# Fused attention and soft-MoE on one core: routing pieces moved ahead of the attention products, a new tail load, a new setup order, a new end and a whole-row relu

## The chip, the cores and the metric

The kernel runs on one core of one Trainium2 chip. The metric is the device time of one execution in microseconds (us). Runs of a kernel are compared in rounds with runs of the kernel before on the same chip. A ratio is the mean time of one kernel's fast runs over the mean of the other's fast runs of the same rounds, so it is not quite the ratio of the medians that stand beside it; the brackets are its 95% interval.

With one core a run is called slow when it is over 1.5% above the fastest of its kernel.

In the profile's lines PE is TensorE and PEld its loading of weights, DVE is VectorE, ACT ScalarE, POOL GpSimd and SP SyncE; a q behind one (ACTq) marks its issuing of loads. L90 is a line of the kernel that was profiled, so numbers shift between kernels. "Granted clock" (PEclk, in tenths on a page) is the share of TensorE's full clock that it was given.

The span in a profile is about 1.7 us shorter than the time of the same run.

## The reference, cut to what matters

```python
# q, k, v: [8 batches, 8 heads, 576, 64]; beacon_k, beacon_v: [8, 8, 16, 64]
k_all, v_all = concat([beacon_k, k]), concat([beacon_v, v])      # along the tokens
a = softmax(mask(q @ k_all.T / 8))                               # causal, beacons always seen
x = (a @ v_all) as [4608 tokens, 512]
logits = x @ phi                                                 # [4608, 32 slots]
d = softmax over the tokens;  slot_input = d.T @ x               # "slot sums"
for e in range(8):                                               # 4 slots each
    slot_out[e] = relu(slot_input[e] @ w1[e]) @ w2[e]            # 512 -> 1024 -> 512
c = softmax over the slots;   out = c @ slot_out                 # [4608, 512]
```

## The kernel before

The loop runs over 32 pairs of heads, four to a batch. In iteration `n` TensorE computes scores of pair `n` (four steps, each followed by ScalarE's exponential), the attention products of pair `n - 1`, and the transposes of q and k for pair `n + 2`. Routing of finished batches is strewn in as pieces: transposes of x, logits, transposed weights, slot sums. The weights of the experts (32 loads of 512 KB) come in during the loop.

```python
for n in range(NP):                      # NP = 32, b = batch, g = pair in the batch
    score(n, 0); score(n, 1)
    ...                                  # n == 0: turning of V, tail, loads 5 and 6
    if n >= 2: xt_piece(n - 2)           # transposes x
    if n >= 1: attend(n - 1)
    score(n, 2)
    if n + 2 < NP:
        transp(n + 2)                    # q and k; same two PSUM buffers as the pieces
        ...
    score(n, 3)
    if n >= 5 and g == 1: logit_piece(b - 1, 0)
    if n >= 6 and g == 2: logit_piece(b - 1, 1)
    if n >= 6 and g == 3: dt_piece(b - 1)
    if n >= 8 and g == 0: si_piece(b - 2)
    ...
# V's last 80 keys ("the tail"), three loads of 32 rows for four batches
def load_tail(b4, i):
    lo = (TK * (16 + i) - Nb) * D
    w = min(TK * D, S * D - lo)
    nc.gpsimd.dma_start(out=vlast[32 * i:32 * i + 32, 0:w],
                        in_=vrows[32 * b4:32 * b4 + 32, lo:lo + w])
...
# relu of an expert's hidden layer: PSUM read in order, two rows written in turn
nc.scalar.activation(hs[e][:, :, :].rearrange("p r f -> p f r"),
                     hpv.rearrange("p (f r) -> p f r", r=2), AF.Relu)
```

The softmax here doesn't subtract the row's maximum and nothing guards it: scores larger than these inputs give would overflow.

## Time and profile before

| | before |
|---|---|
| time, median of the first 3 runs | 213.06 us (210.86 to 216.03) |
| span of the profiled run (fast) | 214.2 us |
| first mask of the fifth iteration starts | 34.03 us |
| iterations 13 to 28, mean | 4.52 us |
| first mask of the last iteration starts | 156.13 us |
| last attention product to first expert layer | 5.89 us |
| expert layers | 21.6 us |
| end of the layers to the end of the span | 27.5 us |

GpSimd's causal mask of 128x1024 follows the first exponential of every iteration, so its 32 starts are a pace-maker: their distance is what an iteration takes. The stages are told with the lines in the prediction.

### The profile page before, as it was taken

How to read it: one execution, taken by the hardware profiler on the slowest of the kernel's cores; microseconds unless marked ns; L12 is line 12 of the kernel's file. 1: busy time of each engine (PE TensorE's matmuls, PEld its weight loads, DVE VectorE, ACT ScalarE, POOL GpSimd, SP SyncE). 2: the span in 40 equal slices, each digit the busy share in tenths (PEclk: the TensorE clock that was granted, in tenths of full speed). 3: DMA queues.
4: the chain of work that ended last, by engine and by line, in shares of the span. 5: the costliest groups of instructions: out<-in, count | busy, mean ns of one | idle time of the engine just before them, and what ended most of it. 6: DMA issues, size and time to landing. Idle time of an engine off the chain costs nothing.

```text
span 214.2 us, 7748 instructions
## 1 busy us (share of the span) xinstructions
PE 155.8 (73%) x3400; PEld 113.4 (53%) x3400; DVE 135.3 (63%) x268; ACT 133.6 (62%) x187; POOL 92.0 (43%) x182
## 2 busy tenths in 40 slices
PE   2438796888868788887877888888886877688200
PEld 1326675767756666665666666677564343233000
DVE  4378589578748878967875797787463121289400
ACT  2226386688767678867767876887851743389300
POOL 8426367645775643756643673346640000000000
PEclk9999699799999999999999999999997555899955
DMA  6999999999999999999999999977999300059996
GB/s 175 269 284 369 242 195 256 252 257 260 311 250 250 271 258 259 314 251 271 259 262 262 281 240 254 205 140 148 197 213 214 67 0 3 0 220 416 416 424 286
DMA packets 20273, 50.88 MB, mean 238 GB/s; under 512 B 5392, under 2 KB 5392, under 8 KB 19216
## 3 DMA queue, kind: packets, MB, share of 16 engines
q0 software_dynamic: 8000, 21.75, 52.3%
q1 hardware_dynamic: 12096, 28.35, 36.9%
q8 instruction: 26, 0.43, 0.7%
q10 hardware_dynamic: 144, 0.29, 0.4%
q14 instruction: 7, 0.06, 0.1%
HBM read 62.69 MB, written 9.44 MB: 337 GB/s over the span
## 4 chain that ended last, share of the span: by engine, by line
PE 39%; DVE 32%; DMA 9%; ACT 6%; issue 6%; SPq 1%; POOL 1%; DVEq 0%; ACTq 0%
PE av L282 12%; DVE xb L290 9%; DVE qT L244 7%; PE sc L255 7%; DMA arena<-in_k_dram 5%; DVE arena L513 5%; PE tr L305 4%; PE tr L316 4%; DMA arena<-in_moe_w_dram 4%; PE av L483 3%; ACT ex L261 3%; DVE vh L135 3%; DVE r L289 3%; ACT hbuf L470 2%; DVE kT L244 2%
## 5 line engine op out<-in xcount | busy, mean ns | idle before, releaser
L261 ACT ACTIVATE ex<-sc 128x1024 f16<-128x1024 f32 (+3 forms) x128 | 103.8, 871 | 36.0 <-PE sc L255 35.2
L263 POOL TENSOR_SCALAR_AFFINE_SELECT ex<-ex 128x1024 f16<-128x1024 f16 x32 | 35.0, 1093 | 62.3 <-ACT ex L261 62.3
L255 PE MATMUL sc<-qT,kT 64*128 64x128 bf16 (+5 forms) x576 | 42.7, 254 | 4.7 <-POOL kT L235 3.0
L282 PE MATMUL av<-vh,ex 128*128 128x65 f16 (+1 forms) x896 | 38.6, 200 | 1.2 <-issue 1.2
L282 PEld LDWEIGHTS <-ex 128*128 128x128 f16 (+2 forms) x960 | 37.0, 110 | 1.9 <-issue 1.6
L242 PE MATMUL tr<-idb,arena 64*64 64x64 bf16 x1152 | 26.9, 198 | 7.7 <-DMA arena<-in_q_dram 3.7
L242 PEld LDWEIGHTS <-arena 64*64 64x64 bf16 x1152 | 22.6, 113 | 15.5 <-issue 9.1
L290 DVE TENSOR_TENSOR xb<-av,r 128x640 f16<-128x640 f32 x32 | 26.4, 824 | 1.1
L244 DVE COPY qT<-tr 128x576 bf16<-128x576 bf16 x32 | 23.9, 747 | 4.6 <-PE tr L242 4.5
L255 PEld LDWEIGHTS <-kT 64*128 64x128 bf16 (+1 forms) x576 | 19.6, 100 | 13.0 <-issue 6.5
L244 DVE COPY kT<-tr 128x576 bf16<-128x576 bf16 x32 | 23.9, 747 | 1.0 <-PE tr L242 1.0
L309 DVE COPY xT<-tr 128x592 f16<-128x592 f16 x32 | 14.6, 456 | 14.4 <-PE tr L305 14.4
L135 DVE STREAM_TRANSPOSE vh<-vbuf 128x512 f32<-128x512 f32 x16 | 17.8, 1128 | 1.5 <-DMA arena<-in_v_dram 1.5
L164 POOL DMA_DIRECT2D arena<-in_moe_w_dram x32 | 17.8, 557 | 0.0
L289 DVE RECIPROCAL r<-av 128x10 f32<-128x10 f32 x32 | 7.1, 220 | 16.3 <-PE av L282 16.3
L316 PE MATMUL tr<-xT,phih 128*128 128x288 f16 x64 | 10.4, 284 | 8.6 <-DVE qT L244 8.4
L111 POOL DMA_DIRECT2D vbuf<-in_v_dram x28 | 15.7, 567 | 0.0
L305 PE MATMUL tr<-idh,xb 128*128 128x128 f16 (+1 forms) x160 | 14.6, 223 | 1.0 <-DVE xb L290 0.9
L320 ACT ACTIVATE eLh<-tr 128x288 f16<-128x288 f32 x16 | 6.6, 412 | 13.6 <-PE tr L316 13.6
L511 ACT ACTIVATE arena<-fp,rc 128x512 f32<-128x512 f32 x18 | 11.3, 685 | 4.0 <-PE fp L509 3.3
L477 DVE COPY hbuf<-tr 128x256 f16<-128x256 f16 x8 | 2.3, 292 | 17.1 <-PE tr L476 17.1
L305 PEld LDWEIGHTS <-xb 128*128 128x128 f16 (+1 forms) x160 | 9.4, 100 | 6.8 <-issue 5.7
(67 smaller groups left out, 152.0 us busy)
## 6 DMA issues: line engine op xcount, KB each, us to landing
arena<-in_moe_w_dram POOLq DMA_DIRECT2D x32, 512.0 KB, 9.4
arena<-in_q_dram SPq DMA_DIRECT2D x32, 288.0 KB, 9.2
arena<-in_k_dram SPq DMA_DIRECT2D x31, 288.0 KB, 11.2
out_dram<-arena SPq DMA_DIRECT2D x8, 1024.0 KB, 8.5
vbuf<-in_v_dram POOLq DMA_DIRECT2D x31, 128.0 KB, 7.5
out_dram<-arena SPq DMA_DIRECT2D x2, 512.0 KB, 3.0
arena<-in_v_dram POOLq DMA_DIRECT2D x4, 128.0 KB, 8.4
arena<-in_k_dram ACTq DMA_DIRECT2D x1, 288.0 KB, 2.8
```

The costliest lines, as they stand in the source:

```text
L111: nc.gpsimd.dma_start(out=vbuf[b % 2][32 * qd:32 * qd + 32, :], in_=bass.AP(tensor=v.tensor, offset=v.offset + lo, ap=[hs_, cs_, [1, TK * ...
L135: nc.vector.transpose(out=dst[:, e], in_=src.bitcast(FP).rearrange("p (j e) -> p e j", j=TK)[:, e])
L164: nc.gpsimd.dma_start(out=arena[:, wloc[m]:wloc[m] + WP], in_=src)
L242: nc.tensor.transpose(tp[po:po + 64, j, :], hi, idb[po:po + 64, po:po + 64])
L244: nc.vector.tensor_copy(out=dst[:, Nb:Nb + S].rearrange("p (s j) -> p s j", j=J), in_=tp[:, :, :].rearrange("p j s -> p s j"))
L255: nc.tensor.matmul(sc[0:kn, a, col:col + un], kT[n % 3][64 * a:64 * a + 64, P * c:P * c + kn], qT[n % 3][64 * a:64 * a + 64, u0:u0 + un], ...
L261: nc.scalar.activation(ex[n][:, :, o:o + w], sc[:, :, 0:w], AF.Exp, scale=scale)
L263: nc.gpsimd.affine_select(out=ex[n][:, :, 0:512].rearrange("p a (c t) -> p a c t", c=4), in_=ex[n][:, :, 0:512].rearrange("p a (c t) -> p ...
L282: nc.tensor.matmul(av[0:m, a, i * DD:(i + 1) * DD], ex[n][0:kn, a, o:o + m], vchunk(b, 2 * g + a, c, kn), start=(c == 0), stop=(c == i))
L290: nc.vector.tensor_tensor(out=xb[b % 2][:, :, 2 * g:2 * g + 2, :].rearrange("p i a d -> p a i d"), in0=avv[:, :, :, 0:D], in1=r5[:, :, :]. ...
L305: nc.tensor.transpose(tp[:, i, 0:m], xb[b % 2][0:m, i, 2 * g:2 * g + 2, :].rearrange("p h d -> p (h d)"), idh[0:m, 0:m])
L316: nc.tensor.matmul(lp[:, 0:w], phih[:, t, :, :].rearrange("p g s -> p (g s)"), xT[b][:, t, Nb + hf * w:Nb + (hf + 1) * w], start=(t == 0), ...
```

## The change

It is meant to take the routing pieces out of the wait for the q and k copies, to shorten the last batch's routing and the layers, and to start loads with fewer instructions. Cut to its core:

```diff
 def load_tail(b4, i):
-    lo = (TK * (16 + i) - Nb) * D
-    w = min(TK * D, S * D - lo)
-    nc.gpsimd.dma_start(out=vlast[32 * i:32 * i + 32, 0:w],
-                        in_=vrows[32 * b4:32 * b4 + 32, lo:lo + w])
+    rows = bass.AP(tensor=v.tensor, offset=...,
+                   ap=[[TK * D, 2], [S * D, 32], [1, TK * D]])
+    if i == 0:
+        nc.gpsimd.dma_start(out=vlast[0:64, :], in_=rows)
+    else:
+        ...                              # the last 32 rows, as before
@@ setup
-    load_pair(3)                         # on SyncE's queue
-    load_pair(4)
@@ n == 0
     load_pair(5)
     load_pair(6)
+    load_pair(3, nc.scalar, nc.scalar)   # issued by ScalarE, behind its first exponentials
+    load_pair(4, nc.scalar, nc.scalar)
+    beacons(1, B)                        # was in n == 1
     ...                                  # first k copies of n < 2 go to VectorE; a memset goes to n == 5
@@ loop
+    if n >= 5 and g in (1, 2): logit_piece(b - 1, g - 1)
+    if n >= 6 and g == 3: dt_piece(b - 1)
     if n >= 1: attend(n - 1)
+    if n >= 6 and g == 3: add_si(b - 1, 0)      # slot sums in halves
+    if n >= 8 and g == 0: add_si(b - 2, 1)
     score(n, 2)
     transp(n + 2) ...
     score(n, 3)
-    ...                                  # the four pieces stood here
@@ end
+    attend(NP - 1, split=True)           # normalisation in two halves
+    ...                                  # last logits in parts, 28 column sums, siz from PSUM
@@ layers
-    nc.scalar.activation(hs[e][:, :, :].rearrange("p r f -> p f r"),
-                         hpv.rearrange("p (f r) -> p f r", r=2), AF.Relu)
+    nc.scalar.activation(hs[e][:, :, :], hpv.rearrange("p (f r) -> p r f", r=2), AF.Relu)
-    if e == 4: col_sums()
+    if e == 1: col_sums(7, NG)
+    # final scaling: first half on ScalarE, second on VectorE
```

More of the change, by code (lines that the diff above doesn't have):

```diff
@@ L83, with load_pair @@
     QKS = 5
-    def load_pair(n, other=None):
+    def load_pair(n, keng=None, qeng=None):
         b, g = divmod(n, H // 2)
@@ L89, in load_pair @@
             t = arena[:, o:o + 2 * J * D].bitcast(FP).rearrange("p (j d) -> p j d", j=J)
-            (other if other is not None and i == 1 else nc.sync).dma_start(
+            ((qeng, keng)[i] or nc.sync).dma_start(
                 out=t,
@@ L127, in load_tail @@
     def load_tail(b4, i):
-        lo = (TK * (16 + i) - Nb) * D
-        w = min(TK * D, S * D - lo)
-        nc.gpsimd.dma_start(out=vlast[32 * i:32 * i + 32, 0:w],
-                            in_=vrows[32 * b4:32 * b4 + 32, lo:lo + w])
+        rows = bass.AP(tensor=v.tensor, offset=v.offset + 32 * b4 * S * D + (16 * TK - Nb) * D,
+                       ap=[[TK * D, 2], [S * D, 32], [1, TK * D]])
+        if i == 0:
+            nc.gpsimd.dma_start(out=vlast[0:64, :], in_=rows)
+        else:
+            lo = (18 * TK - Nb) * D
+            nc.gpsimd.dma_start(out=vlast[64:96, 0:S * D - lo],
+                                in_=vrows[32 * b4:32 * b4 + 32, lo:S * D])
     def turn(dst, src, hf):
@@ L190 @@
         load_v(0, qd)
-    for i in range(3):
+    for i in range(2):
         load_tail(0, i)
@@ L207 @@
     siz = const.tile([P, E, NDC, NSL], F16, name="siz")
-    nc.gpsimd.memset(siz[:, :, :, :], 0.0)
     siacc = const.tile([P, NDC, NSL], FP, name="siacc")
@@ L234, in transp @@
     def transp(n):
-        nc.gpsimd.tensor_copy(out=kT[n % 3][:, 0:Nb], in_=bkT[:, n, :])
+        (nc.vector if n < 2 else nc.gpsimd).tensor_copy(out=kT[n % 3][:, 0:Nb], in_=bkT[:, n, :])
         for (f, dst) in ((qf, qT[n % 3]), (kf, kT[n % 3])):
@@ L272, in score, with attend @@
                 pattern=[[0, 2], [1, UL]], channel_multiplier=-1)
-    def attend(n):
+    def attend(n, split=False):
         b, g = divmod(n, H // 2)
@@ L288, in attend @@
         avv = av[:, :, 0:NCH * DD].rearrange("p a (i d) -> p a i d", d=DD)
-        nc.vector.reciprocal(out=r5[:, :, :], in_=avv[:, :, :, D])
-        nc.vector.tensor_tensor(
-            out=xb[b % 2][:, :, 2 * g:2 * g + 2, :].rearrange("p i a d -> p a i d"),
-            in0=avv[:, :, :, 0:D],
-            in1=r5[:, :, :].unsqueeze(3).broadcast_to([P, 2, NCH, D]), op=AL.mult)
+        xo = xb[b % 2][:, :, 2 * g:2 * g + 2, :].rearrange("p i a d -> p a i d")
+        for z in ((slice(0, 1), slice(1, 2)) if split else (slice(0, 2),)):
+            r_ = r5[:, z, :]
+            nc.vector.reciprocal(out=r_, in_=avv[:, z, :, D])
+            nc.vector.tensor_tensor(
+                out=xo[:, z], in0=avv[:, z, :, 0:D],
+                in1=r_.unsqueeze(3).broadcast_to([P, z.stop - z.start, NCH, D]), op=AL.mult)
     xT = {}
@@ L332, in dt_piece, with si_half @@
         nc.vector.memset(dT[b][0:Nb, 0, :], 0.0)
-    def si_piece(b):
-        sp = ps_tr.tile([P, NDC, NSL], FP, name="tr", tag="tr")
-        for t in range(NDC):
+    def si_half(b, hf):
+        sp = ps_tr.tile([P, 2, NSL], FP, name="tr", tag="tr")
+        for r in range(2):
             for i in range(NCH):
@@ L339, in si_piece, with add_si @@
                 nc.tensor.matmul(
-                    sp[:, t, :],
-                    xb[b % 2][0:m, i, 4 * (t // 2):4 * (t // 2) + 4, :].rearrange(
-                        "p h d -> p (h d)").rearrange("p (f r) -> p f r", r=2)[:, :, t % 2],
+                    sp[:, r, :],
+                    xb[b % 2][0:m, i, 4 * hf:4 * hf + 4, :].rearrange(
+                        "p h d -> p (h d)").rearrange("p (f r) -> p f r", r=2)[:, :, r],
                     dT[b][0:m, i, :], start=(i == 0), stop=(i == NCH - 1))
-        nc.vector.tensor_tensor(out=siacc[:, :, :], in0=siacc[:, :, :], in1=sp[:, :, :],
-                                op=AL.add)
+        return sp[:, :, :]
+    def add_si(b, hf):
+        sp = si_half(b, hf)
+        z = siacc[:, 2 * hf:2 * hf + 2, :]
+        nc.vector.tensor_tensor(out=z, in0=z, in1=sp, op=AL.add)
     beacons(0, 1)
@@ L364 @@
             xt_piece(n - 2)
+        if n >= 5 and g in (1, 2):
+            logit_piece(b - 1, g - 1)
+        if n >= 6 and g == 3:
+            dt_piece(b - 1)
         if n >= 1:
             attend(n - 1)
+        if n >= 6 and g == 3:
+            add_si(b - 1, 0)
+        if n >= 8 and g == 0:
+            add_si(b - 2, 1)
         score(n, 2)
@@ L372 @@
         score(n, 3)
-        if n >= 5 and g == 1:
-            logit_piece(b - 1, 0)
-        if n >= 6 and g == 2:
-            logit_piece(b - 1, 1)
-        if n >= 6 and g == 3:
-            dt_piece(b - 1)
-        if n >= 8 and g == 0:
-            si_piece(b - 2)
         if n == 1:
-            beacons(1, B)
             nc.vector.tensor_copy(out=phih[:, :, :, :],
@@ L390 @@
             load_bv(1)
+        if n == 5:
+            nc.gpsimd.memset(siz[:, :, :, :], 0.0)
         if n == 3:
@@ L404 @@
                 load_bv(b + 2)
-        if 8 <= n < 11:
+        if 8 <= n < 10:
             load_tail(1, n - 8)
@@ L412, with etok, col_sums @@
             wl += 1
-    xt_piece(NP - 2)
-    attend(NP - 1)
-    si_piece(B - 2)
-    xt_piece(NP - 1)
-    logit_piece(B - 1, 0)
-    logit_piece(B - 1, 1)
-    dt_piece(B - 1)
-    si_piece(B - 1)
+    G = 4
+    NG = N // (P * G)
+    csp = scs[1][:, 0, :]
+    rc = const.tile([P, NG * G], FP, name="rc")
+    def etok(cg, j):
+        o = Nb + cg * P * G
+        return eLh[:, o:o + P * G].rearrange("p (t j) -> p t j", j=G)[:, :, j]
+    def col_sums(c0, c1):
+        for i in range(c0 * G, c1 * G):
+            nc.tensor.matmul(csp[:, i:i + 1], etok(i // G, i % G)[0:NSL], ones[0:NSL, :],
+                             start=True, stop=True)
+        z = rc[:, c0 * G:c1 * G]
+        nc.vector.tensor_scalar(out=z, in0=csp[:, c0 * G:c1 * G], scalar1=2.0 ** 8,
+                                scalar2=None, op0=AL.mult)
+        nc.vector.reciprocal(out=z, in_=z)
@@ new lines, with last_logits @@
+    L = B - 1
+    xt_piece(NP - 2)
+    attend(NP - 1, split=True)
+    lps = [scs[0][:, hf, 0:S // 2] for hf in range(2)]
+    def last_logits(ts):
+        for hf in range(2):
+            for t in ts:
+                o = Nb + hf * (S // 2)
+                nc.tensor.matmul(lps[hf], phih[:, t, :, :].rearrange("p g s -> p (g s)"),
+                                 xT[L][:, t, o:o + S // 2],
+                                 start=(t == 0), stop=(t == NDC - 1))
+    add_si(L - 1, 1)
+    nc.vector.tensor_scalar(out=siacc[:, :, :], in0=siacc[:, :, :], scalar1=2.0 ** -8,
+                            scalar2=None, op0=AL.mult)
@@ new lines @@
+    last_logits(range(NDC - 1))
+    xt_piece(NP - 1)
+    last_logits(range(NDC - 1, NDC))
+    for hf in range(2):
+        o = Nb + L * S + hf * (S // 2)
+        nc.scalar.activation(eLh[:, o:o + S // 2], lps[hf], AF.Exp,
+                             accum_out=dsum9[:, 2 * L + hf:2 * L + hf + 1])
+    col_sums(0, 7)
+    dt_piece(L)
+    ds = siz[:, :, :, :]
+    for hf in range(2):
+        sp = si_half(L, hf)
+        for r in range(2):
+            c = 2 * hf + r
+            nc.vector.scalar_tensor_tensor(
+                out=bass.AP(tensor=ds.tensor, offset=ds.offset + c * NSL,
+                            ap=[ds.ap[0], [NDC * NSL + SPE, E], [1, SPE]]),
+                in0=sp[:, r, :].rearrange("p (e s) -> p e s", e=E), scalar=2.0 ** -8,
+                in1=siacc[:, c, :].rearrange("p (e s) -> p e s", e=E),
+                op0=AL.mult, op1=AL.add)
@@ L427 @@
     nc.vector.reciprocal(out=rd[:, :], in_=dsum[:, :])
-    ds = siz[:, :, :, :]
-    nc.vector.tensor_scalar(
-        out=bass.AP(tensor=ds.tensor, offset=ds.offset,
-                    ap=[ds.ap[0], [NDC * NSL + SPE, E], [NSL, NDC], [1, SPE]]),
-        in0=siacc[:, :, :].rearrange("p c (e s) -> p e c s", e=E),
-        scalar1=2.0 ** -8, scalar2=None, op0=AL.mult)
-    G = 4
-    NG = N // (P * G)
-    def etok(cg, j):
-        o = Nb + cg * P * G
-        return eLh[:, o:o + P * G].rearrange("p (t j) -> p t j", j=G)[:, :, j]
-    rc = const.tile([P, NG * G], FP, name="rc")
-    def col_sums():
-        csp = ps_tr.tile([P, 512], FP, name="tr", tag="tr")
-        for cg in range(NG):
-            for j in range(G):
-                i = cg * G + j
-                nc.tensor.matmul(csp[:, i:i + 1], etok(cg, j)[0:NSL], ones[0:NSL, :],
-                                 start=True, stop=True)
-        nc.vector.tensor_scalar(out=rc[:, :], in0=csp[:, 0:NG * G], scalar1=2.0 ** 8,
-                                scalar2=None, op0=AL.mult)
-        nc.vector.reciprocal(out=rc[:, :], in_=rc[:, :])
     sop = av[:, 0, :]
@@ L491 @@
             turn_hidden(e - 1)
-        if e == 4:
-            col_sums()
+        if e == 1:
+            col_sums(7, NG)
         if e > 1:
@@ L496 @@
     soh = const.tile([P, Dm], F16, name="soh")
-    nc.vector.tensor_scalar(out=soh[:, :], in0=sop[:, :], scalar1=rd[:, 0:1],
+    nc.scalar.activation(soh[:, 0:Dm // 2], sop[:, 0:Dm // 2], AF.Copy, scale=rd[:, 0:1])
+    nc.vector.tensor_scalar(out=soh[:, Dm // 2:Dm], in0=sop[:, Dm // 2:Dm], scalar1=rd[:, 0:1],
                             scalar2=None, op0=AL.mult)
```

## The prediction

> **What bounds the kernel now.** I read the page first, for the stages:
>
> ```profile
> PE   2438796888868788887877888888886877688200
> DVE  4378589578748878967875797787463121289400
> ACT  2226386688767678867767876887851743389300
> ...
> PEclk9999699799999999999999999999997555899955
> DMA  6999999999999999999999999977999300059996
> ```
>
> Four stages show. To about 20 us the core waits for first loads. From 20 to 160 us the attention loop runs, with TensorE the busiest engine and the DMA engines full. From 160 to 188 us come the last batch's routing and the expert layers, at a granted clock of 0.5. From 188 us on the output stage is full of DMA again. Since 9.44 MB leave at about 416 GB/s (22.7 us), that last stage can't shrink; it can only start earlier.
>
> Next, the waits by line (total, times, longest):
>
> ```profile
> PE tr L316 <- DVE qT L244: 8.4, 13, 0.7
> ...
> PE tr L328 <- DVE qT L244: 3.8, 6, 0.9
> ...
> PE av L483 <- ACT hbuf L470: 3.3, 3, 1.1
> ...
> PE sc L255 <- POOL kT L235: 3.0, 1, 3.0
> ...
> PE tr L339 <- DVE qT L244: 2.2, 4, 0.7
> ```
>
> L316, L328 and L339 are the routing pieces (logits, transposed weights, slot sums). Each stands behind the q and k transposes, which use the same two PSUM buffers, so TensorE waits about 0.65 us until VectorE has evacuated q: 14.4 us in all. Two whole iterations without a piece, by the timeline:
>
> ```profile
> 28.26 0.86 PE L255 MATMUL sc<-qT,kT 64*128 64x128 bf16 x14 [0.15 <-ACT ex L261]
> ...
> 31.82 0.87 PE L255 MATMUL sc<-qT,kT 64*128 64x128 bf16 x14 [0.15 <-ACT ex L261]
> ```
>
> Their score products start 3.56 us apart, and ScalarE's exponentials release both: 3.56 us is what the loop costs without routing. With pieces, the first masks of successive iterations around 120 to 150 us stand 4.2 to 4.5 us apart, a batch of four 17.4 us.
>
> The timeline of the end:
>
> ```profile
> 159.28 0.22 DVE L289 RECIPROCAL r<-av 128x10 f32<-128x10 f32 x1 [0.59 <-PE av L282]
> 159.53 0.82 DVE L290 TENSOR_TENSOR xb<-av,r 128x640 f16<-128x640 f32 x1
> ...
> 161.73 0.41 ACT L320 ACTIVATE eLh<-tr 128x288 f16<-128x288 f32 x1 [3.46 <-PE tr L316]
> ...
> 165.12 1.42 PEld L465 LDWEIGHTS <-siz 128*32 128x32 f16 x32 [1.07 <-DVE siz L429]
> ...
> 166.30 1.31 ACT L470 ACTIVATE hbuf<-sc 128x256 f16<-128x256 f32 x1 [3.58 <-PE sc L465]
> ...
> 172.59 1.04 PE L483 MATMUL av<-arena,hbuf 128*32 128x512 f16 x8 [1.08 <-ACT hbuf L470]
> ...
> 174.75 1.36 PE L448 MATMUL tr<-ones,eLh 32*128 32x1 f16 x36
> ```
>
> The last attention ends at 159.1, the layers start at 165.1: 6 us of one short step after another. A relu of 256 columns takes 1.31 us though an exponential of 288 takes 0.41, and every second second-layer waits 1.1 us for one.
>
> [...] In one-us windows the clock is 1.00 to 163, 0.50 from 164 to 183 and 1.00 from 184[...]. [...]
>
> **The change, part by part.** (1) Loop. Logits go ahead of attention, right after the x^T transposes. The 0.65 us buffer wait goes; in its place the fourth of four products waits for the x^T copy (0.47 us, started on time), about 0.2 us, and ScalarE's 0.41 us lies in time in which it waits for scores. Iteration: 3.56 + 0.58 of TensorE work = 4.1 us against 4.4 now, 0.3 saved, twice per batch. The transposed weights move ahead too (0.65 saved), but in the same iteration half a slot sum (0.3) comes in, and its VectorE addition stands behind the 0.82 us normalisation; the k transposes use its buffer and wait about 0.4. Nearly nothing saved there. In the fourth iteration half the sum goes, and 0.55 of wait becomes about 0.5: 0.3 saved. Sum per batch: 0.3 + 0.3 + 0.05 + 0.3 = 0.95 us, by 6.75 batches 6.4 us. So of 14.4 us of waits I count less than half.
>
> (2) Head. The first k copy moves to VectorE and saves 2 us of the 3.0 there (kT done at 6.6, score at 8.66). But the next gate is the loads: V landed about 13.4, the third q at 14.5, and the 224 KB of beacon keys 11.0 us after their issue, at 13.7. Their cast and copies (1.13 + 0.79 us of VectorE), taken ahead of V's turning, push the first attention from 17.5 to about 20.4. The second iteration then lacks the 2.17 us stall for them. ScalarE, with four loads put between its first exponentials, whose issue waits for earlier loads to land, is held to about 17 to 19 us. I get the third pair's first exponential at 24 to 24.3 against 24.34: 0 us.
>
> (3) Last routing. Splitting the last normalisation gives x about 0.45 us earlier. Three of four logit products are done before the last x^T; the softmax sums (0.16 + 0.15 + 0.16 and gaps, 0.65 us) leave the path, and siz is written straight from PSUM. 28 column sums (about 36 ns each, 1.0 us) come in, half hidden behind the exponentials, but their 0.58 us of VectorE work stands ahead of the weights' copy. Net, layers start 5.2 us after the last attention instead of 6.0: 0.9 saved.
>
> (4) Layers. Relu 1.31 to about 0.4: the three waits of 1.1 become 0.25 (2.55), the first 0.64 goes: 3.2. Column sums 36 to 8: 1.0. Together 4.2 of the 21.6 us at the clock of today.
>
> (5) Clock. With those gaps gone, layers at half clock are 90% dense[...]. An expert costs 2.16 us of TensorE at half clock (0.86 + 0.33 + 0.97) and about 1.3 at full clock: 0.43 (half), 0.22 and 0.5 (as the last expert, at full clock, shows them) and half a relu wait. Warm for six experts gains 5 us, for none 0, for all 6. I take 3.
>
> (6) The split of the final scaling: the built order has VectorE's half waiting for ScalarE's, so 0. Fewer load instructions and the later memset on GpSimd: off the path, 0.
>
> Sum: 6.4 + 0 + 0.9 + 4.2 + 3 = 14.5 us.
>
> **Rivals.** *DMA takes over the loop.* Per batch 2.36 MB of q and k at about 390 GB/s (the rate at 15 to 20 us) take 6.1 us, and 2.3 MB of V and weights at 210 GB/s (the rate at 150 to 160 us, where only they move) 11.1: 17.2 us, as an estimate, against my 16.5 per batch. For it: DMA full in every slice, loads landing 7 to 14 us after issue. Against: TensorE hardly waits for q today (1.9 us in 9 waits), and five pairs of prefetch, some 20 us, can absorb a lag of 5. If it binds, the loop saves 2: 205.
> *VectorE takes over.* In the third and fourth iterations of a batch it already has 3.9 to 4.4 us of work with V's turning, and the slot sums' buffer then waits longer. For it: VectorE is 9 tenths busy in some slices. The loop saves 3: 204.
> *TensorE takes all it waits for.* All 14.4 us come back as the pieces hide: 192 to 194. Against it stands ScalarE's 3.56 us.
> *The clock stays low* to the output: 203.
> *The head gets worse*, since ScalarE blocks on the issue of loads: 2 us lost, 202.
>
> **Range and chances.** The time before is 213.06 as median of 210.86 to 216.03. I take off 14.5 and give back 2 for the first two rivals: 200.5 us. Range 195 to 207: below, hidden pieces and a warm clock together; above, DMA pace and cold layers together. Faster by over 2% means below 208.8: 0.93; within 2% 0.06; slower 0.01.
>
> **What will show it.** The relus should read near 0.4 us, and the waits of L483 on them 0.2 or less. The three waits on the q copy should be gone, with new ones on the x^T copy (logits) and on the slot addition (k transposes); batches should be 16.5 us apart late in the loop. The first layer should start 5.2 us after the last attention and the layers last 13 to 17. The clock's row tells part 5. I'm wrong if the loop keeps its 17.4 us per batch with waits on q, k or V loads, or if the first attention is later than 21 us and nothing makes that up.

## More of the kernel before

One more view of this kernel: what the tail loads took. The lines give count, duration of the issue in ns (min/median/max), first and last start, and then the time from issue to landing.

```profile
L130 POOL DMA_DIRECT2D arena<-in_v_dram x6: 494/503/560, 5.0 to 63.8; - x6
...
DMA to landing us min/median/max: 7.3/8.2/8.8
```

## The result, and the profile after

The changed kernel is correct and slower: 222.31 us as median of four runs (221.70 to 224.13), against 214.55 (210.86 to 216.66, four runs), ratio 1.0502 [1.0362, 1.0643]. The profiled run was fast, with a span of 220.8 us.

Three rows of the changed kernel's page, by slices of 5.5 us (before's stand in the prediction):

```profile
ACT  2300176879558875745797676788778422279400
...
PEclk9999999999969996995999999999999988999855
DMA  6995539999999999999999999999799990039996
```

Two things stand out. Slices three to five hold almost no ScalarE work (0 0 1), and DMA's row falls to 5 5 3 in slices four to six, where before it was all 9: the head is broken. And the clock's row shows 8 8 9 in the layers (180 to 193 us), where before it fell to 5.

Where the 6.6 us of span went, from the mask starts and the stage ends of both traces:

| stage | before | after | difference |
|---|---|---|---|
| start to the fifth iteration's mask | 34.03 | 43.31 | +9.28 |
| fifth to thirteenth mask | 37.64 | 42.45 | +4.81 |
| thirteenth to 29th mask (16 iterations) | 72.25 | 72.28 | +0.03 |
| 29th to 32nd mask | 12.21 | 13.33 | +1.12 |
| last mask to end of the last attention product | 3.11 | 3.52 | +0.41 |
| last attention product to the first layer | 5.89 | 5.56 | -0.33 |
| layers | 21.61 | 12.76 | -8.85 |
| final scaling | 0.88 | 1.04 | +0.16 |
| output | 26.58 | 26.55 | -0.03 |

The waits of the changed kernel (total us, times, longest us) name the first two rows:

```profile
ACT ex L262 <- DMA arena<-in_k_dram: 17.2, 1, 17.2
...
DVE arena L139 <- DMA arena<-in_v_dram: 4.9, 1, 4.9
...
POOL vbuf L150 <- DMA arena<-in_v_dram: 3.9, 1, 3.9
...
PE tr L319 <- DVE xT L312: 0.9, 5, 0.2
```

L319 are the logits: their 8.4 us of waits for the q copy have become 0.9 us for the x^T copy. So the change did to these waits what it was meant to do, while the pace in the table's third row did not move.

ScalarE's timeline in the head (start, duration, engine, line; ACTq is the issue of a load):

```profile
7.35 1.91 ACT L262 ACTIVATE ex<-sc 128x1024 f16<-128x1024 f32 x2 [4.82 <-PE sc L256]
14.44 0.33 ACTq L90 DMA_DIRECT2D arena<-in_q_dram  x1
17.99 0.34 ACTq L90 DMA_DIRECT2D arena<-in_k_dram  x1
24.71 0.33 ACTq L90 DMA_DIRECT2D arena<-in_q_dram  x1
26.12 0.33 ACTq L90 DMA_DIRECT2D arena<-in_k_dram  x1
26.50 1.35 ACT L262 ACTIVATE ex<-sc 128x928 f16<-128x928 f32 x2 [17.24 <-DMA arena<-in_k_dram]
```

Two exponentials end at 9.26; then ScalarE issues four loads one by one, each 0.02 us after the last part of an earlier load landed (14.42, 17.96, 24.69 and 26.10 us, by the landings in the packed trace), and the next exponential starts only at 26.50. Behind it stand loads that land late. The tail load (L131) and the DMA in windows (busy us of PE, PEld, DVE, ACT and POOL, each with its count, then the granted clock, the mean share of the 16 DMA engines and GB/s):

```profile
L131 POOL DMA_DIRECT2D arena<-in_v_dram x2: 677/686/695, 5.0 to 63.9; - x2
...
DMA to landing us min/median/max: 17.9/18.2/18.6
```

```profile
20.00:21.00 1.00, 0.00 (x0) 0.00 (x0) 0.00 (x0) 0.00 (x0) 0.00 (x0) 1.00 0.25 87
21.00:22.00 1.00, 0.01 (x2) 0.01 (x2) 0.00 (x0) 0.00 (x0) 0.00 (x0) 1.00 0.13 40
22.00:23.00 1.00, 0.97 (x20) 0.68 (x21) 0.00 (x0) 0.00 (x0) 0.00 (x0) 1.00 0.20 50
```

For comparison the kernel before in one of these windows:

```profile
21.00:22.00 1.00, 0.00 (x0) 0.00 (x0) 1.00 (x3) 0.37 (x1) 1.00 (x3) 1.00 0.99 195
```

The tail load takes 18.2 us where its predecessors took 8.2, and toward its end a share of 0.13 of the DMA engines moves, which is two of 16. Loads of another queue that were still on their way are late as well: the third q landed 14.8 us after its issue instead of 11.2, the small table of phi 20.5 instead of 11.4 (three loads of V issued just ahead of the tail 9.6 instead of 8.9).

The packed trace lists every single DMA packet, and it shows how (these are not lines of a view). From 15.3 to 17.8 us a packet of phi starts every 311 ns, and 7 ns after each a packet of the tail, which takes 322: that reads as the two taking turns on one engine (a packet's record has no engine). In the run with the new tail alone (below) five or six packets of the tail start in each us from 14 to 19, 1.6 to 1.9 us of packet time in a us, so two engines' worth.

The same trace has the landings, and each load lands in 16 parts. In the changed kernel 14 parts of the tail load are there by 15.92 us and the last two come at 19.80 and 23.58; of phi 14 by 15.62, the last two at 20.56 and 24.69; of the q load issued at 6.85, 14 by 16.35, the last two at 21.23 and 25.40. Before, the 16 parts of phi came between 12.25 and 15.77, those of the q load issued at 7.11 between 13.36 and 16.37.

That suggests a cause outside the prediction. The old load has 32 rows on both sides. The new one has 2 on the source's side, ahead of its rows, and 64 rows on the other. That this leading 2 puts the load on two of the 16 engines was at this point my estimate, from the share of 0.13 and the two late parts.

The end answers to the prediction's timeline of before:

```profile
180.20 0.48 DVE L472 SCALAR_TENSOR_TENSOR siz<-tr,siacc 128x32 f16<-128x32 f32 x4 [0.58 <-PE tr L342]
180.45 1.41 PEld L497 LDWEIGHTS <-siz 128*32 128x32 f16 x32 [0.20 <-DVE siz L472]
...
181.63 0.39 ACT L502 ACTIVATE hbuf<-sc 128x256 f16<-128x256 f32 x1 [2.96 <-PE sc L497]
...
184.14 0.61 PE L514 MATMUL av<-arena,hbuf 128*32 128x512 f16 x8
```

The relu takes 0.39 us instead of 1.31, and the second layer (L514) no longer waits for one.

### The profile page after: what moved, and what is told of

The parts are those of the page before. It is cut to its first block, busy times and chain, and to the rows that moved or that the text cites.

```text
span 220.8 us, 7754 instructions
## 1 busy us (share of the span) xinstructions
PE 161.6 (73%) x3400; PEld 118.1 (53%) x3400; DVE 136.4 (62%) x284; ACT 128.3 (58%) x188; POOL 91.2 (41%) x178
## 2 busy tenths in 40 slices
DMA packets 21137, 50.88 MB, mean 230 GB/s; under 512 B 6256, under 2 KB 6256, under 8 KB 20080
## 4 chain that ended last, share of the span: by engine, by line
DMA 34%; PE 31%; DVE 14%; ACT 8%; issue 4%; POOL 2%; DVEq 0%; SPq 0%; ACTq 0%
DMA vbuf<-in_beacon_v_dram 10%; DMA arena<-in_k_dram 8%; PE av L283 8%; DMA arena<-in_v_dram 8%; ACT ex L262 7%; PE sc L256 7%; DMA vbuf<-in_v_dram 6%; DVE arena L545 5%; PE tr L243 4%; PE tr L308 3%; DVE xb L294 2%; PE av L514 2%; DVE vh L139 2%; DMA arena<-in_q_dram 1%; DVE xT L312 1%
## 5 line engine op out<-in xcount | busy, mean ns | idle before, releaser
L262 ACT ACTIVATE ex<-sc 128x1024 f16<-128x1024 f32 (+3 forms) x128 | 105.6, 870 | 59.8 <-PE sc L256 40.4
L256 PE MATMUL sc<-qT,kT 64*128 64x128 bf16 (+5 forms) x576 | 46.8, 259 | 14.6 <-ACT ex L262 12.6
L283 PEld LDWEIGHTS <-ex 128*128 128x128 f16 (+2 forms) x960 | 38.9, 112 | 4.8 <-issue 3.0
L243 PE MATMUL tr<-idb,arena 64*64 64x64 bf16 x1152 | 29.8, 203 | 9.5 <-DMA arena<-in_k_dram 4.5
L256 PEld LDWEIGHTS <-kT 64*128 64x128 bf16 (+1 forms) x576 | 21.8, 102 | 24.3 <-issue 19.9
L243 PEld LDWEIGHTS <-arena 64*64 64x64 bf16 x1152 | 24.6, 117 | 18.9 <-issue 10.4
L294 DVE TENSOR_TENSOR xb<-av,r 128x640 f16<-128x640 f32 (+1 forms) x33 | 26.5, 804 | 1.1
L293 DVE RECIPROCAL r<-av 128x10 f32<-128x10 f32 (+1 forms) x33 | 7.1, 215 | 27.9 <-PE av L283 27.8
L168 POOL DMA_DIRECT2D arena<-in_moe_w_dram x32 | 17.9, 559 | 3.9 <-DMA arena<-in_moe_w_dram 2.6
L139 DVE STREAM_TRANSPOSE vh<-vbuf 128x512 f32<-128x512 f32 x16 | 17.9, 1135 | 1.8 <-DMA vbuf<-in_beacon_v_dram 1.8
L545 DVE TENSOR_SCALAR arena<-fp,rc 128x512 f32<-128x512 f32 x18 | 12.3, 746 | 0.7 <-PE fp L541 0.7
L541 PE MATMUL fp<-soh,eLh 128*128 128x512 f16 x36 | 10.6, 377 | 2.6 <-ACT arena L543 1.4
L319 PE MATMUL tr<-xT,phih 128*128 128x288 f16 x56 | 10.4, 295 | 1.2 <-DVE xT L312 0.9
```

The costliest lines, as they stand in the source:

```text
L139: nc.vector.transpose(out=dst[:, e], in_=src.bitcast(FP).rearrange("p (j e) -> p e j", j=TK)[:, e])
L168: nc.gpsimd.dma_start(out=arena[:, wloc[m]:wloc[m] + WP], in_=src)
L243: nc.tensor.transpose(tp[po:po + 64, j, :], hi, idb[po:po + 64, po:po + 64])
L256: nc.tensor.matmul(sc[0:kn, a, col:col + un], kT[n % 3][64 * a:64 * a + 64, P * c:P * c + kn], qT[n % 3][64 * a:64 * a + 64, u0:u0 + un], ...
L262: nc.scalar.activation(ex[n][:, :, o:o + w], sc[:, :, 0:w], AF.Exp, scale=scale)
L283: nc.tensor.matmul(av[0:m, a, i * DD:(i + 1) * DD], ex[n][0:kn, a, o:o + m], vchunk(b, 2 * g + a, c, kn), start=(c == 0), stop=(c == i))
```

## The experiments

The letters: T says that the tail load's form, by its few DMA engines, costs the time; S that ScalarE, blocked by its four load issues, does; Q that the new places in the loop gain nothing, because pieces ahead of the attention products delay scores that ScalarE needs. Other letters are spelled out in the expectations in which they stand. "Old tail" means the three 32-row loads of before.

**Old tail in the changed kernel.** Only `load_tail` and its calls go back.

```diff
-    rows = bass.AP(..., ap=[[TK * D, 2], [S * D, 32], [1, TK * D]])   # one load of 64 rows
+    vlast[32 * i:32 * i + 32, 0:w]  <-  vrows[32 * b4:..., lo:lo + w]  # for i in 0, 1, 2
```

> The changed kernel with V's tail loaded by three DMAs of 32 rows again, all else as changed. Theory T (the one DMA of two blocks of 32 rows sits on few DMA engines, and all loads that share those engines land late): the 18 us landings go back to 8 or 9, the loads issued by ScalarE no longer block it to 26 us but to about 17 to 19, first attention near 20.5, time near 203 to 207. Theory S (ScalarE's four load issues block it by themselves): ScalarE still waits past 24 us, time stays above 217. Theory R (the new routing places cost the time in the loop): 218 or more too.

Measured: 212.54 us (211.21 to 212.79), ratio 0.9867 [0.9779, 0.9955]: T's landings (8.1 us), but 5 us or more above T's time, since the loop's gain is missing (below). The mask of the second iteration starts at 20.55 us instead of 29.24. ScalarE still issues the four loads, but now it is free at 17.8:

```profile
17.81 1.35 ACT L258 ACTIVATE ex<-sc 128x928 f16<-128x928 f32 x2 [8.17 <-DMA arena<-in_q_dram]
```

**Pairs 3 and 4 back on SyncE's queue, the new tail kept.**

```diff
-    load_pair(3, nc.scalar, nc.scalar); load_pair(4, nc.scalar, nc.scalar)   # n == 0
+    load_pair(3); load_pair(4)                                               # in the setup
```

> The changed kernel with pairs 3 and 4 loaded by SyncE in the setup again, the two-block tail load kept. Theory T: the tail still lands at about 24 us and VectorE still waits for it, and the second tail load still blocks GpSimd near 80 us: 216 to 222, little gained. Theory S: the head is mended, about 210.

Measured: 218.54 us (218.09 to 218.96), ratio 1.0158 [1.0076, 1.0241]; the second mask starts at 26.11. So ScalarE's queue carries part of the damage, but only on top of late loads: the same move onto the kernel before shows nothing, as the run after next tells.

**New tail alone in the kernel before.**

```diff
-    vlast[32 * i:32 * i + 32, 0:w]  <-  vrows[32 * b4:..., lo:lo + w]  # for i in 0, 1, 2
+    vlast[0:64, :]  <-  bass.AP(..., ap=[[TK * D, 2], [S * D, 32], [1, TK * D]])   # and the last 32
```

> The kernel before with only the tail loads changed (one of two blocks of 32 rows and one of 32 rows). Theory T: loses 8 to 14 us, 222 to 228, with loads landing 15 to 18 us after issue in the head. Theory S: as before, 213.

Measured: 226.59 us (224.17 to 228.31), ratio 1.0494 [1.0306, 1.0683]; second mask 24.95 instead of 17.86, and a step of 9.13 us to the thirteenth, behind the second such load. This part alone loses as much as the whole change. That both ratios are near 1.05 is chance: the changed kernel also wins 8.6 us at its end, and the tail takes it from 0.9867 to 1.0502.

**ScalarE's queue alone in the kernel before.**

```diff
-    load_pair(3); load_pair(4)                                               # in the setup
+    load_pair(3, nc.scalar, nc.scalar); load_pair(4, nc.scalar, nc.scalar)   # n == 0
```

> The kernel before with only pairs 3 and 4 moved behind pairs 5 and 6 and on to ScalarE's queue. Theory T: 0 to 3 us worse, since ScalarE is held to about 17 to 19 us, when V's turning ends anyway. Theory S: 8 us or more worse.

Measured: 216.23 us (215.68 to 216.79), ratio 1.0051 [0.9966, 1.0137]: nothing that can be told from zero.

**The two outer dimensions exchanged.** Same bytes, same number of instructions, same length of rows; only the count that leads on the source's side changes from 2 to 32. Rows land in another order, so the result is wrong.

```diff
-    ap=[[TK * D, 2], [S * D, 32], [1, TK * D]])
+    ap=[[S * D, 32], [TK * D, 2], [1, TK * D]])
```

> The changed kernel with one thing edited: in the 64-row tail load the two outer dimensions of the source change places (32 rows of stride S*D first, then the 2 blocks), so bytes, number of load instructions, descriptors and their length stay, and only the leading count goes from 2 to 32. The result is wrong on purpose (rows of the tail land in another order). T (the leading 2 leaves most DMA engines idle): the tail load lands some 8 us after its issue instead of 17 to 18.6, the first mask of the second iteration starts near 20.5 us instead of 29.2, the second tail load no longer holds GpSimd 3.9 us, and the time is that of the changed kernel with the three old tail loads, 210 to 214. Rival: it is the size of one load (256 KB in one instruction, or fewer instructions) that delays it; then nothing moves and the time stays 219 to 225.

Measured: 213.35 us (212.11 to 216.58), ratio 0.988 [0.973, 1.0031], the same as with the old tail. The profiled run is the one at 216.58 and counts as slow; its tail load reads

```profile
L131 POOL DMA_DIRECT2D arena<-in_v_dram x2: 562/572/582, 5.0 to 55.1; - x2
...
DMA to landing us min/median/max: 8.1/9.5/10.9
```

against 17.9 to 18.6 in the changed kernel. The rival, the size of one load, falls: 256 KB in one instruction is fine with 32 leading rows, and the DMA share from 18 to 21 us is 1.01 where the changed kernel has 0.65 and then 0.25. T is shown from both sides and by the one number that was changed here. One thing besides the order of rows differs: the kernel with the leading 2 has 896 more packets on its page (21137 against 20241), all of 4 bytes. They come with the form and weren't tested apart; at 9 ns each (the median of the 4-byte packets in the changed kernel's packed trace) they make about 0.5 us for each of 16 engines in both tail loads together, an estimate, against some 9 us of delay.

**Loop places alone in the kernel before.** The pieces go to the new places, nothing else changes.

```diff
+    logit_piece / dt_piece               # ahead of attend(n - 1)
     attend(n - 1)
+    add_si in halves                     # behind it
     score(n, 2) ... score(n, 3)
-    logit_piece / dt_piece / si_piece
```

> The kernel before with only the loop's routing pieces moved (logits and weights ahead of attention, slot sums in halves). Theory P, from the prediction (the wait of TensorE for the q copy is lost time): 6 us faster, 208 where before has 214. Theory Q (that wait lay beside ScalarE's last two exponentials of the iteration, and a piece ahead of attention delays the third score and leaves ScalarE idle 0.8 us before it): no gain or a loss of 1 to 4 us, with batches 17.4 us apart or more.

Measured: 219.44 us (217.87 to 263.73), ratio 1.0185 [1.003, 1.034]; the profiled run was slow (263.73, one of four).

**The changed kernel with the old order of loads and beacons** (old tail, pairs 3 and 4 on SyncE, beacons late), so only loop and end are new. In this run, the next one and the one with the single final scaling, the first k copies stay on VectorE.

```diff
-    one tail load of 64 rows; load_pair(3 and 4, nc.scalar, nc.scalar); beacons(1, B) at n == 0
+    three tail loads of 32 rows; load_pair(3 and 4) in the setup; beacons(1, B) at n == 1
```

> The changed kernel with the whole order of loads and beacons of before (three tail loads, pairs 3 and 4 on SyncE in the setup, beacons in the second iteration); new places in the loop, new end, new relu. If only the head and tail loads were at fault: 204 or less. If the loop's new places cost what the head's order wins: as the run with the old tail loads, 210 to 213.

Measured: 213.39 us (209.92 to 213.81, no ratio given, since three of the four runs lie over 1.5% above the fourth).

**The same with the old places in the loop too**, so the end, the relu and the column sums are new.

```diff
-    pieces ahead of and behind attend(n - 1), slot sums one half at a time
+    pieces behind score(n, 3), both halves of the slot sum at g == 0
```

> As the run before it, and the loop's routing pieces at their old places too, so the end, the relu and the column sums alone are new. Theory Q: 205 to 207, since the end and the layers won about 8 us in the profile of the changed kernel and nothing is lost elsewhere. Theory P: slower than the run before it by 6 us.

Measured: 210.37 us (209.23 to 211.62), ratio 0.9789 [0.9676, 0.9901], above the 205 to 207 that were expected. That is 3 us under the run before by the medians, but three of that one's four runs count as slow, and its fast one (209.92) is no worse: nothing is shown here about the places.

**Only the relu in the kernel before.**

```diff
-    nc.scalar.activation(hs[e][:, :, :].rearrange("p r f -> p f r"),
-                         hpv.rearrange("p (f r) -> p f r", r=2), AF.Relu)
+    nc.scalar.activation(hs[e][:, :, :], hpv.rearrange("p (f r) -> p r f", r=2), AF.Relu)
```

> The kernel before with only the relu's access pattern changed to whole rows written. The relu falls from 1.31 to 0.39 us; at the clock of 0.5 that wins about 3 us, and 5 to 8 if the clock comes back sooner[...].

Measured: 209.1 us (208.3 to 210.6), ratio 0.9737 [0.963, 0.9843]. One of before's relu groups, then the same of this run (min/median/max ns):

```profile
L470 ACT ACTIVATE hbuf<-sc x4: 1307/1329/1422, 166.3 to 181.4; 128x256 f16<-128x256 f32 x4
```

```profile
L470 ACT ACTIVATE hbuf<-sc x4: 384/384/384, 166.0 to 175.6; 128x256 f16<-128x256 f32 x4
```

By these medians the old form takes (1329 - 384) / 256 = 3.7 ns a column more, an estimate: it writes 2 bytes in turn into two rows 256 bytes apart, where the new one writes whole rows and reads every second float of PSUM.

The layers fall from 21.6 to 13.9 us, and the clock's row of this run shows why that is more than the relus' waits:

```profile
PEclk9999799999999969999999999999999969999955
```

Where before has 5 5 5 8 from 166 us on, it has 6 9 9 from 165: with the relus at 384 ns most of the layers had 0.9 of the clock or more. This one line gives nearly all that the good parts of the change give together.

**New head with the old tail, old places, new end.** The changed kernel with two parts taken back.

```diff
-    one tail load of 64 rows; pieces ahead of and behind attend(n - 1)
+    three tail loads of 32 rows; pieces behind score(n, 3)
```

> The changed kernel with the three old tail loads and the old places of the routing pieces in the loop; the new order of the head (two pairs behind others on ScalarE's queue, beacon casts early, first k copies on VectorE), the new end and the relu stay. If the head is worth what it seemed to be (select of the fifth iteration about 1 us earlier, given back in the next one by late V): 210, as with the old head (210.4). If the gain holds once the loop has its old places: 209. If ScalarE's issue waits cost more than that: 212 or more.

Measured: 210.19 us (208.87 to 212.52), ratio 0.9732 [0.9573, 0.9891]; with the old head it was 210.37. The reordered head is worth nothing that shows. Against the changed kernel with the old tail (0.9867 [0.9779, 0.9955]) it differs in the loop's places alone; the intervals overlap.

**Old head, old places, new end, one final scaling on VectorE.**

```diff
-    nc.scalar.activation(soh[:, 0:Dm // 2], ..., AF.Copy, scale=rd[:, 0:1])
-    nc.vector.tensor_scalar(out=soh[:, Dm // 2:Dm], ...)
+    nc.vector.tensor_scalar(out=soh[:, :], in0=sop[:, :], scalar1=rd[:, 0:1], ...)
```

> The kernel before with only the relu, the column sums spread out and the new routing of the last batch; the final scaling on VectorE alone again (the split cost 0.16 us). From the stages: before 214 to 218, layers and end 26.6+0.9 then 12.8 layers and 5.6 routing: 8.9 us less in layers, 0.25 in the routing: ratio 0.958 to 0.98, 0.1 to 0.2 us better than with the split, within noise. Best of all runs if the stage sums hold; against the relu alone (0.974) about 1 us better by the layers (13.9 to 12.8), which two runs have not shown in the total.

Measured: 209.44 us (207.19 to 211.67), before in the same rounds 217.79, ratio 0.9683 [0.9493, 0.9873]. It has the lowest ratio of all correct kernels, but its interval covers that of the relu alone, as do those of the two kernels above it: by the totals the new end isn't told from nothing, though its stages are 1.2 us shorter in the layers and 0.2 in the routing. In its trace the layers take 12.67 us and the final scaling 0.88 (1.04 with the split).

**Loop places alone, a second time**.

> The kernel before with only the loop's new places, run again, since the profile of its first run fell in the slow state. Q (pieces ahead delay the score that ScalarE needs): ratio 1.00 to 1.03 again, ScalarE's idle time before the exponentials that wait for score products above that of before (36 us), batches of 17.4 to 17.8 us late in the loop. P (the first run was the DMA's noise): ratio 0.98 to 1.00 and batches of 17.0 or less.

Measured: 218.74 us (216.14 to 223.74), ratio 1.0072 [0.9779, 1.0365]; the profile is again one of a run called slow. Together with the first: no gain, and a loss of at most a few per cent.

What made the new places gain nothing was still open: DMA, as the prediction's first rival, or the engines. Four runs set both in a table. All have the whole-row relu. Their outputs are wrong, which doesn't matter for the times.

**No routing pieces in the loop at all.**

```diff
-    logit_piece / dt_piece / si_piece    # in the loop
+    nc.vector.memset(eLh[:, :], 0.5); nc.vector.memset(dsum9[:, :], 1.0)   # in the setup
```

> The kernel before with the whole-row relu and without any routing piece in the loop (no logits, weights, slot sums of the first seven batches; wrong result on purpose). With the pieces the same kernel takes 209 and its loop 4.56 us an iteration. D (DMA sets the pace): the loop stays at 4.3 us an iteration or more, the time at 203 or more. E (the engines set it): iterations near 3.6 us, as the two without a piece early in the loop of before, some 20 us less, time 188 to 195.

Measured: 206.26 us (205.54 to 208.86), ratio 0.9639 [0.9486, 0.9792]. Against the 0.9737 of the relu alone (from other rounds; the intervals overlap), all routing in the loop, work and waits, is worth about 1% of the time. In the two traces the last mask starts 5.1 us earlier without it (151.10 against 156.23), and routing, layers and output take 2.2 of that back. So taking the pieces out altogether wins less in the loop than the 6.4 us that new places were to win.

**Weight loads of half the bytes, old places.**

```diff
-    nc.gpsimd.dma_start(out=arena[:, wloc[m]:wloc[m] + WP], in_=src)
+    nc.gpsimd.dma_start(out=arena[:, wloc[m]:wloc[m] + WP // 2], in_=src[:, 0:WP // 2])
```

(Each half is used twice, so the work on the engines stays.)

> The kernel before with the whole-row relu, and with weight loads of half the bytes (each half used twice, wrong result on purpose), old places of the routing pieces. D: the loop gets faster, by up to a sixth of what the DMA moves in it, 4.56 to about 4.2 us an iteration, time 200 to 204. E: pace as with whole loads, 207 to 210.

Measured: 203.44 us (201.91 to 205.74), ratio 0.9494 [0.9317, 0.9672].

**The same with the new places.** Half the bytes, and the loop of the changed kernel as in the test of the loop places.

> As the one before, with the new places of the pieces in the loop. D with a right step 1: freed from the DMA, the new places gain their 0.95 us a batch over the old ones, time 4 to 7 us under that of the old places. E: same as the old places or up to 3 us slower, with ScalarE's waits for score products higher.

Measured: 209.98 us (209.82 to 210.18), ratio 0.9827 [0.9678, 0.9976]: 6.5 us slower than with the old places, more than E's 3, and the two intervals don't touch.

**Half the bytes and no pieces.** Both edits above together.

> Half the weight bytes and no pieces at all: what the loop takes with neither. D and E both: near 3.6 us an iteration; if it is much above, a third thing (VectorE with V's turning, or loads of q, k and V alone) sets the pace.

Measured: 195.76 us, one run; its loop takes 4.07 us an iteration, not near 3.6.

The mean of iterations 13 to 28, from the mask starts (the profiled runs of the middle and lower row are fast or, for the one without pieces at half bytes, single):

| us per iteration | no pieces | old places | new places |
|---|---|---|---|
| weights whole, before and after | - | 4.52 | 4.52 |
| weights whole, whole-row relu | 4.53 | 4.62 | - |
| weights half | 4.07 | 4.31 | 4.55 |

The same stretch by the windows view, columns as above, of relu alone, then no pieces, then half the bytes with old places, then half the bytes and no pieces:

```profile
70.00:144.00 74.00, 61.34 (x1565) 48.82 (x1562) 57.27 (x108) 55.55 (x82) 39.39 (x77) 0.98 1.02 253
```

```profile
67.00:140.00 73.00, 59.77 (x1446) 46.77 (x1446) 55.90 (x92) 53.47 (x66) 39.52 (x79) 0.93 1.06 268
```

```profile
70.00:139.00 69.00, 58.39 (x1564) 47.26 (x1561) 56.94 (x108) 54.47 (x82) 39.31 (x77) 1.00 0.87 203
```

```profile
66.00:131.00 65.00, 54.43 (x1433) 42.45 (x1432) 54.01 (x91) 52.67 (x65) 39.31 (x77) 1.00 0.91 220
```

A share a little over 1 is to be read as full. With whole weights the DMA engines are full and the pace is 4.5 to 4.6 us whether the pieces are there or not; with half, they are 87% busy and it drops to 4.31. So the loads hold this loop back. How much is less sure. Each cell is one trace; fast traces with old places and whole weights go from 4.42 (new tail alone) to 4.77 (old head with the new end), and without pieces the granted clock was lower, 0.93 against 0.98. And the loads don't set every step: with half the bytes and old places the steps from mask to mask repeat 4.38, 4.39, 4.38 and 4.02 us, 17.2 a batch, which reads as the engines' own rhythm with the pieces. By this comparison whole weights add 0.2 to 0.3 us an iteration, as single long steps. Only without pieces does TensorE itself stand for loads (3.8 us in 3 waits for k in that stretch; none for k in the relu run).

With half the bytes the pieces count: taking them away gains another 0.24 us an iteration (one run). What holds the loop at 4.07 then is open; its last four steps, when the loads of q and k are over, are 3.56 us each.

But the new places lose 0.24 there instead of gaining. With whole weights too: from the 29th to the 32nd mask, when the loads of q and k are over, every fast trace with the new places takes 13.05 to 13.33 us, every one with the pieces in the old places 12.20 to 12.63. Where, show ScalarE's groups in that stretch (count, busy us, mean ns, then idle before it and the releaser), first old places, then new:

```profile
L261 ACT ACTIVATE ex<-sc 128x1024 f16<-128x1024 f32 x17 | 17.4, 1023 | 9.2 <-PE sc L255 9.2
...
L261 ACT ACTIVATE ex<-sc 128x928 f16<-128x928 f32 x16 | 15.2, 952 | 0.0
...
L320 ACT ACTIVATE eLh<-tr 128x288 f16<-128x288 f32 x8 | 3.3, 410 | 6.2 <-PE tr L316 6.2
```

```profile
L261 ACT ACTIVATE ex<-sc 128x1024 f16<-128x1024 f32 x16 | 16.4, 1022 | 0.9
L261 ACT ACTIVATE ex<-sc 128x928 f16<-128x928 f32 x16 | 15.1, 943 | 13.3 <-PE sc L255 13.3
L261 ACT ACTIVATE ex<-sc 128x416 f16<-128x416 f32 x16 | 8.3, 517 | 2.6 <-PE sc L255 2.2
```

In the old places ScalarE idles about 15 us in 16 iterations: before the first exponential of an iteration (9.2) and before the logits' (6.2), both behind pieces that waited for the q copy. In the new places these are gone, and ScalarE idles 16.8 (0.9 + 13.3 + 2.6), nearly all before the third exponential (928 columns): the piece now stands between the second and the third score step, together with the transposes of x and the attention products. The first two exponentials cover only 2.0 us of that (1022 + 995 ns). The wait has changed its place and its name. These lines don't hold the whole loss: ScalarE idles 2.3 us more by the windows view (69.0 less 54.5 busy, 72.7 less 55.9), and the 16 iterations take 3.8 us longer.

## Why the prediction was wrong

It said 200.5 us with 0.93 for faster; the kernel is 5% slower. By its own steps:

*(6), "Fewer load instructions ... off the path, 0": this is the step that failed.* I counted the new tail load as fewer instructions and didn't look at its access pattern. At the thirteenth mask the changed kernel is 14.1 us behind (85.76 against 71.67), and with the old tail 1.4 (73.05): the form costs 12.7, in the head and again behind its second issue, where GpSimd stood 3.9 us. Giving back the old form gains 0.9867 against 1.0502; the form alone gives 1.0494; exchanging two dimensions is as good as the old form. That the leading 2 was the cause is shown by the exchange (landings of 8.1 and 10.9 us instead of 17.9 and 18.6). For phi the packets stand 7 ns ahead of the tail's, one each 311 ns; that the other late loads were held in the same way is my reading of the 0.13 and of their two late parts, and no run isolates it.

*(2), the head, 0.* With the old tail the step's own numbers hold: ScalarE held to 17.8 (I said 17 to 19), first attention at 19.8 (20.4), and the fifth mask at 33.02 instead of 34.03; one iteration later late V loads take that back. The head of the changed kernel without the tail is worth 0, as said. What I mis-saw was its fragility: with loads late, ScalarE's issue order turns 8.2 us of blocking into 17.2, which moving the loads back shows (1.0158 against 1.0502).

*(1), the loop, 6.4 us: wrong too.* The term that was mis-sized is "3.56 us is what the loop costs without routing". The engines can do it: two iterations did early on, and the last four of the run with half the bytes and no pieces. But over 16 iterations without any piece the loop takes 4.53 with whole weights and 4.07 with half. That fits my first rival, that DMA takes over the loop, at 18.1 us for a batch (4 x 4.53), where I had estimated 17.2 and given it two of 6.4 us. And even with DMA relieved the new places lose, since I followed TensorE's waits and not what ScalarE does while TensorE waits. I predicted the new waits on the x^T copy (0.9 us in 5) and on the slot addition rightly, and they say nothing about the pace.

*(3), last routing, 0.9.* 0.33, of which the later end of the last attention product (0.41) takes all back. The built order has half a slot sum and the transposed weights ahead of that product.

*(4) and (5), layers, 4.2 + 3 = 7.2.* 8.85: relu 0.39 us, the layers at 0.8 to 0.9 of the clock. The relu alone makes 7.7 of it, the column sums 1.15 (13.91 to 12.76), where I had 1.0. These were right, and a little small. What brings the clock back, on which (5) rests, isn't shown here. In the packed traces of before and after every stretch at one clock, ahead of the last, takes 3.41 us or a multiple of it. In the last 3.4 us before the clock fell to 0.50, at 163.2, TensorE was busy for 2.03 and never idle for 1 us. Over a stretch without a gap of TensorE from 173.4 to 178.3 (busy for 4.86) the clock stayed at 0.50; after one from 180.2 to 183.7 (busy for 3.50) it was 1.00.

*(6), split of the final scaling, 0.* It costs 0.16.

So of my 14.5 us, 8.6 came (8.85 + 0.33 - 0.41 - 0.16), the 6.4 of the loop did not (its late iterations lost 1.1 instead), and 14.1 (9.3 + 4.8) came on top, 12.7 of it from a part that I had put at nothing.

## What to carry to other kernels

Read the access pattern of every changed load, not only its bytes and count: here a leading 2 on the source's side landed in 18.2 us, at a DMA share that fell to 0.13, and a leading 32 with the same bytes in 8.1 and 10.9, and that cost more than everything else gained. Before moving waits within a loop, take the moved work out altogether once: what that gains is the most that another order of the pieces can win. A wait counts only where the engine that sets the pace stands idle with it: here TensorE's waits at the logits went from 8.4 us to 0.9, and the 16 iterations from 72.25 us to 72.28.
